# Attention denominators through a row of memory: one broadcast transfer per head instead of four row copies and two shuffles

## The chip, the cores and the metric

The kernel runs on one core of a Trainium2 chip. The metric is the device time of one execution in microseconds (us). A core has five engines that run their own instruction streams and wait for each other through semaphores: TensorE (PE in the profile; its weight loads are PEld), VectorE (DVE), ScalarE (ACT), GpSimd (POOL) and SyncE (SP). In this kernel every transfer is issued by SP, in one queue, and carried by 16 DMA engines.

## The reference

For each batch b and head, queries and keys are projected by `w_phi`, the row's largest absolute value is subtracted, and exp of plus and minus the result gives 256 features:

```python
def phi(x):
    proj = np.einsum('bhsd,df->bhsf', x, w_phi)
    proj = proj - np.max(np.abs(proj), axis=-1, keepdims=True)
    return np.concatenate([np.exp(proj), np.exp(-proj)], axis=-1)
q_p, k_p = (phi(q), phi(k))
kv = np.einsum('bhsf,bhsd->bhfd', k_p, v)
z = np.sum(k_p, axis=2)
num = np.einsum('bhsf,bhfd->bhsd', q_p, kv)
den = np.einsum('bhsf,bhf->bhs', q_p, z)[..., None] + 1e-06
attn = num / den
```

There are 8 batches, 8 heads, 576 positions and a head width of 64. The heads side by side form x, 576 x 512 a batch, which goes through a gated layer: `h = relu(x @ w_in)` (1024 wide), a convolution of width 3 along the positions, a sigmoid of it as the gate, and `(h * gate) @ w_out`. The change concerns the division `num / den` and how its result reaches `x @ w_in`.

## The kernel before

Matrices that need more precision than one pass of TensorE gives are split in a high and a low part (`split`, L56 to L65: the high part by one engine, the rest `src - hi` by another), and a product is three passes.

**Attention.** Heads come in pairs: a tile of 128 partitions holds two heads of 64. A batch has 4 pairs p, two for each half qd of the heads. `k_process` and `q_process` work on groups of columns (five a half, g). The keys' features times v accumulate into `kv`; the queries' features times `kv` give PSUM tiles `nm` of 65 rows, of which 64 are numerators and the 65th is the denominators, because v has a column of ones. ACT copies the numerators to the tile `num` (L459) and the row of denominators to `dr` (L454); a transfer lays that row out as `den`, 72 partitions of 16 (L457): row r of 16 positions of head i stands on partition 2r + i, so that VectorE needs no more than 16 columns for 1152 numbers.

**The division, one process a pair (`x_process`, L464).** VectorE adds 1e-6 (L472) and takes reciprocals into `rc`, 72 x 16 (L473). Then the 576 reciprocals of a head must stand beside each of its 64 partitions of `num`. Four transfers (L477, two a head) write the row of a head to partitions 64i and 64i + 32 of one tile `rr`, which all pairs share. For each chunk c of 290 columns, `stream_shuffle` (L485) spreads the first partition of each 32 over the other 31 into `xf`, which has two buffers, a multiplication by `num` follows (L486), ACT makes the high part `xh` (L60) and VectorE the low part `xl` (L65). There are 8 buffers each of `xh` and `xl`; a new chunk takes one that an earlier part of the gated layer has finished reading.

**Gated layer.** Batch b and chunk c make part n = 2b + c, 16 in all. `h_part` runs 96 matmuls (8 outputs f, 4 pairs, 3 passes) of `xh`, `xl` with `w_in` into `hp`, and ACT applies relu into `h` (L517). `conv_process` does the convolution on POOL (L534) and VectorE (L539), the sigmoid on ACT (L543; it needs another activation table than exp, so a table load of ACT stands before it and before the next exp), the gate product on VectorE (L548), and a split into `gh`, `gl`. `o_part` runs 96 matmuls with `w_out` into `op`; ACT copies them to `os` (L577), which SP stores (L578).

**What sets the order.** The processes are Python generators, and a planner at the end of the function steps attention and gated layer in turn by a clock of its own. That gives the order in which instructions are written down; `tc.high_priority()` moves marked ones ahead. The tile framework then orders each engine's instructions once more by a model of the timeline, places the waits, and each engine runs its list strictly in order. An instruction that waits holds up everything behind it on its engine; a transfer that waits holds up SP's queue. Among the transfers that other work waits for are the rows of maxima `qx<-qmp` (L380), which TensorE's third query pass needs (L386), and the loads `qr`, `kr`, `v`.

Of the kernel before, what the change touches and what calls it, by code (L numbers as in the profile page):

```python
# [7 lines left out]
F32 = mybir.dt.float32  # L8
# [4 lines left out]
ALU = mybir.AluOpType  # L13
AX = mybir.AxisListType.X

B, H, S, D = 8, 8, 576, 64
F = 128
DM, FF = 512, 1024
P = 128
NQ = 2  # L20
TC = 288
HW = TC + 2
# [13 lines left out]
def kernel(  # L36
# [13 lines left out]
    nc = tc.nc  # L50
    cp = ctx.enter_context(tc.tile_pool(name="cp", bufs=1))
    sb = ctx.enter_context(tc.tile_pool(name="sb", bufs=1))
    pg = ctx.enter_context(tc.tile_pool(name="pg", bufs=4, space=bass.MemoryType.PSUM))
    pm = ctx.enter_context(tc.tile_pool(name="pm", bufs=2, space=bass.MemoryType.PSUM))
    pk = ctx.enter_context(tc.tile_pool(name="pk", bufs=1, space=bass.MemoryType.PSUM))

    def split(src, hi, lo, eng_hi, eng_lo):

        if eng_hi is nc.scalar:
            nc.scalar.activation(out=hi, in_=src, func=AF.Copy)  # L60
        elif eng_hi is nc.gpsimd:
            nc.gpsimd.tensor_scalar(out=hi, in0=src, scalar1=1.0, scalar2=0.0, op0=ALU.mult, op1=ALU.add)  # L62
        else:
            nc.vector.tensor_copy(out=hi, in_=src)
        eng_lo.tensor_tensor(out=lo, in0=src, in1=hi.bitcast(F32), op=ALU.subtract)  # L65
# [16 lines left out]
    wq_lo = cp.tile([P, F], F32R, name="wq_lo")  # L82

    wq_m = cp.tile([P, F], F32R, name="wq_m")


    rr = cp.tile([P, S], F32, name="rr")
    nc.gpsimd.memset(rr, 0.0)
    for i in range(2):
        r = slice(D * i, D * i + D)  # L90
        nc.gpsimd.tensor_copy(out=wq_hi[r, :], in_=wbd_hi[r, i * F : (i + 1) * F].bitcast(F32))
    nc.gpsimd.tensor_copy(out=wq_m, in_=rr[:, 0:F])
    nc.gpsimd.tensor_copy(out=wq_lo, in_=rr[:, 0:F])
    nc.gpsimd.tensor_copy(out=wq_lo[0:D, :], in_=wbd_lo[0:D, 0:F].bitcast(F32))
    nc.gpsimd.tensor_scalar(out=wq_m[D : D + 2, :], in0=rr[D : D + 2, 0:F], scalar1=-1.0, scalar2=0.0, op0=ALU.add, op1=ALU.add)
    mx = [cp.tile([32, 32], F32, name=f"mx{i}") for i in range(2)]
    for t in mx:
        nc.gpsimd.memset(t, 0.0)
# [69 lines left out]
    def pe(ns):  # L168
        return ("pe", ns)
# [4 lines left out]
    def until(*keys):  # L174
        return ("until", [k for k in keys if k is not None])

    def set_ready(key, ns=0):
        ready[key] = now[0] + ns * LAT
# [150 lines left out]
    xh, xl = {}, {}  # L329

    def q_process(b, qd, g):
# [129 lines left out]
        if g == 2 or g == 4:  # L461
            spawn(x_process(b, qd * 2 + g // 2 - 1))

    def x_process(b, p):  # L464
        yield ("wait", 4000)
        qd, pr = divmod(p, 2)
        dn, nt = den[b, qd, pr], numt[b, qd, pr]
        if 4 * b + p > 0:
            yield until(("x", *divmod(4 * b + p - 1, 4), 1))
        with tc.high_priority():  # L470
            rc = sb.tile([72, 16], F32, name=f"rc{b}_{p}", tag="rc", bufs=2)
            nc.vector.tensor_scalar(out=dn, in0=dn, scalar1=1e-6, scalar2=None, op0=ALU.add)  # L472
            nc.vector.reciprocal(out=rc, in_=dn)  # L473
            for i in range(2):
                for j in range(2):
                    row = D * i + 32 * j
                    nc.sync.dma_start(out=rr[row : row + 1, :].rearrange("o (r c) -> o r c", c=16),  # L477
                                      in_=rc.rearrange("(r i) c -> i r c", i=2)[i])
        yield ("wait", 4500)
        for c in range(2):  # L480
            yield until(("h", 2 * (b - 1) + c) if b > 0 else None)
            t0 = 0 if c == 0 else S - HW
            with tc.high_priority():
                xf = sb.tile([P, HW], F32, name=f"xf{b}_{p}_{c}", tag="xf", bufs=2)
                nc.vector.stream_shuffle(out=xf, in_=rr[:, t0 : t0 + HW], mask=[0] * 32)  # L485
                nc.vector.tensor_tensor(out=xf, in0=nt[:, t0 : t0 + HW], in1=xf, op=ALU.mult)  # L486
                xh[b, p, c] = sb.tile([P, HW], F32R, name=f"xh{b}_{p}_{c}", tag="xh", bufs=8)
                xl[b, p, c] = sb.tile([P, HW], F32R, name=f"xl{b}_{p}_{c}", tag="xl", bufs=8)
                split(xf, xh[b, p, c], xl[b, p, c], nc.scalar, nc.vector)
            set_ready(("x", b, p, c), 2500)  # L490
            yield pe(125)

# [149 lines left out]
    while moe is not None or chains or active:  # L642
        while chains and sum(1 for p in active if p[2]) < WINDOW:
            b, x, g, kind = chains.pop(0)
# [3 lines left out]
            p = active[-1]  # L648
# [10 lines left out]
        if can_a and (a_first or not can_m):  # L659
            p = active[can_a[0]]  # L660
# [66 lines left out]
```

## Time and profile before

| | |
|---|---|
| median of 3 runs | 825.85 us (825.42 to 827.12) |
| the profiled execution's own time | 827.25 us |
| its span, first to last instruction | 825.5 us |
| mean granted TensorE clock | 0.981 |
| PE busy | 775.8 us, 94% |
| DVE busy | 649.4 us, 79% |
| ACT busy | 627.4 us, 76% |
| POOL busy | 316.1 us, 38% |
| transfers | 55.35 MB by SP's queue, 23.3% of the 16 DMA engines' span |

Busy time is a union over the span, and an engine's share of it is an average over stages: the first 200 us hold the filling of the pipeline and the preparation of the weights, the middle holds attention and gated layer side by side, and from about 720 us only the gated layer is left. "PEclk" is the share of the TensorE clock that was granted. In the trace's rows, `<-` names the tile that is read after the one that is written, and a releaser in brackets is what ended the idle time before an instruction.

### The profile page before, as it was taken

How to read it: one execution, taken by the hardware profiler on the slowest of the kernel's cores; microseconds unless marked ns; L12 is line 12 of the kernel's file. 1: busy time of each engine (PE TensorE's matmuls, PEld its weight loads, DVE VectorE, ACT ScalarE, POOL GpSimd, SP SyncE). 2: the span in 40 equal slices, each digit the busy share in tenths (PEclk: the TensorE clock that was granted, in tenths of full speed). 3: DMA queues.
4: the chain of work that ended last, by engine and by line, in shares of the span. 5: the costliest groups of instructions: out<-in, count | busy, mean ns of one | idle time of the engine just before them, and what ended most of it. 6: DMA issues, size and time to landing. Idle time of an engine off the chain costs nothing. (4 is left out here: it accounts for less than half of the span.)

```text
span 825.5 us, 17295 instructions
## 1 busy us (share of the span) xinstructions
PE 775.8 (94%) x5972; PEld 744.0 (90%) x5972; DVE 649.4 (79%) x1378; ACT 627.4 (76%) x1372; POOL 316.1 (38%) x395
## 2 busy tenths in 40 slices
PE   6988889899999999999999999999999899999997
PEld 5866789798989889999989999999999899999997
DVE  5898999796887968889788798788888587766451
ACT  4787886859898797988888888798988779744322
POOL 5765564262524424344243352525335232211120
PEclk9998989989999999999999999999999899999999
DMA  5544422212222122222222222222222111000001
GB/s 168 179 131 122 130 65 70 66 37 68 67 64 74 38 84 68 68 71 66 78 68 65 69 70 63 70 61 74 62 81 59 51 39 31 10 30 30 22 23 43
DMA packets 66814, 56.44 MB, mean 68 GB/s; under 512 B 17832, under 2 KB 64680, under 8 KB 66728
## 3 DMA queue, kind: packets, MB, share of 16 engines
q1 hardware_dynamic: 66728, 55.35, 23.3%
q8 instruction: 47, 0.77, 0.4%
q14 instruction: 39, 0.32, 0.1%
HBM read 45.21 MB, written 9.44 MB: 66 GB/s over the span
## 5 line engine op out<-in xcount | busy, mean ns | idle before, releaser
L279 PEld LDWEIGHTS kv<-v,ke 128*128 128x128 f32 x1024 | 156.5, 195 | 10.8 <-ACT ke L260 5.2
L279 PE MATMUL kv<-v,ke 128*128 128x65 f32 x1024 | 161.4, 256 | 4.3 <-ACT ke L260 4.2
L539 DVE SCALAR_TENSOR_TENSOR c<-h,cw,c 128x288 f32<-128x288 f32 (+1 forms) x256 | 144.7, 574 | 23.1 <-POOL c L534 21.1
L534 POOL TENSOR_SCALAR c<-h,cw 128x288 f32<-128x288 f32 x128 | 82.3, 645 | 207.2 <-ACT h L517 142.7
L572 PE MATMUL op<-gh,wout_hi 128*128 128x288 f32 x512 | 153.0, 299 | 5.9 <-ACT os L577 5.0
L509 PE MATMUL hp<-xh,win_hi 128*128 128x290 f32 x512 | 154.2, 302 | 4.2 <-ACT h L517 3.3
L572 PE MATMUL op<-gl,wout_hi 128*128 128x288 f32 x512 | 152.3, 298 | 0.9 <-DVE gl L65 0.9
L509 PE MATMUL hp<-xl,win_hi 128*128 128x290 f32 x512 | 153.1, 299 | 0.1
L509 PE MATMUL hp<-xh,win_lo 128*128 128x290 f32 x512 | 152.7, 298 | 0.0
L572 PE MATMUL op<-gh,wout_lo 128*128 128x288 f32 x512 | 152.0, 297 | 0.0
L200 POOL TENSOR_TENSOR qx<-qr,qx 64x512 fp32r<-64x512 f32 (+1 forms) x60 | 77.6, 1294 | 111.2 <-ACT qx L199 102.3
L65 DVE TENSOR_TENSOR ql<-qe,qh 128x512 fp32r<-128x512 f32 x112 | 90.0, 822 | 22.0 <-ACT qh L60 21.7
L509 PEld LDWEIGHTS hp<-xh,win_hi 128*128 128x128 f32 x512 | 97.6, 191 | 7.5 <-ACT h L517 5.4
L572 PEld LDWEIGHTS op<-gh,wout_hi 128*128 128x128 f32 x512 | 97.0, 190 | 7.5 <-ACT os L577 5.9
L572 PEld LDWEIGHTS op<-gl,wout_hi 128*128 128x128 f32 x512 | 97.1, 190 | 1.7 <-DVE gl L65 1.2
L509 PEld LDWEIGHTS hp<-xl,win_hi 128*128 128x128 f32 x512 | 97.9, 191 | 0.7 <-DVE xl L65 0.2
L509 PEld LDWEIGHTS hp<-xh,win_lo 128*128 128x128 f32 x512 | 97.7, 191 | 0.5
L572 PEld LDWEIGHTS op<-gh,wout_lo 128*128 128x128 f32 x512 | 97.2, 190 | 0.5
L62 POOL TENSOR_SCALAR kxh<-kr 128x256 fp32r<-128x256 f32 (+1 forms) x80 | 42.3, 529 | 130.8 <-issue 62.6
L517 ACT ACTIVATE h<-hp 128x290 f32<-128x290 f32 x128 | 50.8, 405 | 40.1 <-PE hp L509 39.6
L432 PE MATMUL nm<-ql,kvh 128*65 128x256 f32 x224 | 69.5, 310 | 0.2 <-DVE ql L65 0.2
L432 PE MATMUL nm<-qh,kvl 128*65 128x256 f32 x224 | 69.2, 309 | 0.0
(99 smaller groups left out, 1879.3 us busy)
## 6 DMA issues: line engine op xcount, KB each, us to landing
qr<-in_qT_dram SPq DMA_DIRECT2D x112, 128.0 KB
v<-in_vt_dram SPq DMA_DIRECT2D x80, 130.0 KB
out_dram<-os SPq DMA_DIRECT2D x64, 144.0 KB
kr<-in_kT_dram SPq DMA_DIRECT2D x64, 128.0 KB
w_r<-in_w_in_dram SPq DMA_DIRECT2D x8, 512.0 KB
w_r<-in_w_out_dram SPq DMA_DIRECT2D x8, 512.0 KB
rr<-rc SPq DMA_DIRECT2D x128, 2.2 KB
qr<-in_qT_dram SPq DMA_DIRECT2D x28, 64.0 KB
```

Of the source, the lines that this page charges most:

```text
L62: nc.gpsimd.tensor_scalar(out=hi, in0=src, scalar1=1.0, scalar2=0.0, op0=ALU.mult, op1=ALU.add)
L65: eng_lo.tensor_tensor(out=lo, in0=src, in1=hi.bitcast(F32), op=ALU.subtract)
L200: nc.gpsimd.tensor_tensor(out=x[D:P], in0=raw[D:P], in1=x[D:P].bitcast(F32), op=ALU.subtract)
L279: ins = nc.tensor.matmul(out=kp[i][:, s, p0 : p0 + VW], lhsT=lhsT, rhs=v[:, (2 * t + i) * VW : (2 * t + i + 1) * VW], start=False, stop=(g ...
L432: ins = after(ins, lambda: nc.tensor.matmul(out=ps[:, i, o : o + w], lhsT=w_, rhs=x_, start=(k == 0), stop=(k == 5)))
L509: nc.tensor.matmul(out=ps, lhsT=w_, rhs=x_, start=(k == 0), stop=(k == 11))
L517: nc.scalar.activation(out=h4[:, f % 4, :], in_=ps, func=AF.Relu)
L534: nc.gpsimd.tensor_scalar(out=cv, in0=hs[:, o : o + TC], scalar1=cw[:, f, 1:2], scalar2=0.0, op0=ALU.mult, op1=ALU.add)
L539: nc.vector.scalar_tensor_tensor(out=cv[:, lo:hi], in0=hs[:, o + j - 1 + lo : o + j - 1 + hi], scalar=cw[:, f, j : j + 1], in1=cv[:, lo:hi ...
L572: nc.tensor.matmul(out=ps, lhsT=w_, rhs=x_, start=(k == 0), stop=(k == 23))
```

## The change

The tile `rr` goes (a tile of zeros for the set-up takes its place there). The reciprocals of a pair are written by one transfer to `rd`, a tile of 2 x 576 in the chip's main memory with two buffers; the address pattern undoes the layout of `rc`, in pieces of 16 numbers. For each head one transfer reads its row back, repeated onto 64 partitions of `rb`, 128 x 576 in SBUF, two buffers. The shuffles go. One multiplication for the whole pair writes `num * rb` into `rb`, and the splits of the two chunks read slices of `rb`.

```diff
-    rr = cp.tile([P, S], F32, name="rr")
+    dp = ctx.enter_context(tc.tile_pool(name="dp", bufs=2, space=bass.MemoryType.DRAM))
+    zero = cp.tile([P, F], F32, name="zero")
...
             nc.vector.reciprocal(out=rc, in_=dn)
+            rd = dp.tile([2, S], F32, name=f"rd{b}_{p}", tag="rd", bufs=2)
+            nc.sync.dma_start(out=rd.rearrange("i (r c) -> r i c", c=16), in_=rc)
+            rb = sb.tile([P, S], F32, name=f"rb{b}_{p}", tag="rb", bufs=2)
             for i in range(2):
-                for j in range(2):
-                    row = D * i + 32 * j
-                    nc.sync.dma_start(out=rr[row : row + 1, :].rearrange("o (r c) -> o r c", c=16),
-                                      in_=rc.rearrange("(r i) c -> i r c", i=2)[i])
+                nc.sync.dma_start(out=rb[D * i : D * i + D, :], in_=rd[i : i + 1, :].broadcast_to([D, S]))
         yield ("wait", 4500)
         for c in range(2):
             yield until(("h", 2 * (b - 1) + c) if b > 0 else None)
             t0 = 0 if c == 0 else S - HW
             with tc.high_priority():
-                xf = sb.tile([P, HW], F32, name=f"xf{b}_{p}_{c}", tag="xf", bufs=2)
-                nc.vector.stream_shuffle(out=xf, in_=rr[:, t0 : t0 + HW], mask=[0] * 32)
-                nc.vector.tensor_tensor(out=xf, in0=nt[:, t0 : t0 + HW], in1=xf, op=ALU.mult)
+                if c == 0:
+                    nc.vector.tensor_tensor(out=rb, in0=nt, in1=rb, op=ALU.mult)
                 xh[b, p, c] = sb.tile([P, HW], F32R, name=f"xh{b}_{p}_{c}", tag="xh", bufs=8)
                 xl[b, p, c] = sb.tile([P, HW], F32R, name=f"xl{b}_{p}_{c}", tag="xl", bufs=8)
-                split(xf, xh[b, p, c], xl[b, p, c], nc.scalar, nc.vector)
+                split(rb[:, t0 : t0 + HW], xh[b, p, c], xl[b, p, c], nc.scalar, nc.vector)
```

Because the framework orders the instructions anew, they move on every engine. Three places follow. A name such as `xh_1_0_9527` is pair 1, chunk 0 of its batch and then the tile's own number (the batch is left out); the changed file is one line longer at the top, so L66 there is the L65 of before and L61 the L60. In brackets stand the semaphores that the instruction waits for; those named DMAHW belong to transfers.

**ScalarE, batch 6, pairs 0 and 1**, where their chunks are split. Before:

```order
1017 L60 ACTIVATE xh_0_0_9220<-xf_0_0_9217 128x290 [waits PE_49]
1018 L60 ACTIVATE xh_0_1_9227<-xf_0_1_9224 128x290 [waits PE_49]
1019 L517 ACTIVATE h_4_8675<-hp_7_8705 128x290 [waits PE_49]
1020 L60 ACTIVATE xh_1_0_9527<-xf_1_0_9524 128x290 [waits DVE_49]
1021 L371 ACTIVATE qmt_0_2_9272<-qmt_0_2_9272 32x16 [waits DVE_49]
1022 L371 ACTIVATE qmt_0_2_9272<-qmt_0_2_9272 32x16 x2
1023 L60 ACTIVATE xh_1_1_9534<-xf_1_1_9531 128x290 [waits DVE_49]
1024 L543 ACT_TABLE_LOAD
1025 L543 ACTIVATE c_9068<-c_9068 128x2304 [waits DVE_49]
1026 L399 ACT_TABLE_LOAD
```

Now:

```order
1027 L61 ACTIVATE xh_0_0_9125<-rb_0_8937 128x290 [waits PE_49]
1028 L399 ACTIVATE qe_0_2_0_9528<-qp_0_2_9171 128x512 [waits DVE_49]
1029 L61 ACTIVATE xh_0_1_9129<-rb_0_8937 128x290 [waits PE_49]
1030 L61 ACTIVATE xh_1_0_9428<-rb_1_9244 128x290 [waits PE_49]
1031 L399 ACTIVATE qe_0_2_1_9532<-qp_0_2_9171 128x512 [waits DVE_49]
1032 L61 ACTIVATE xh_1_1_9432<-rb_1_9244 128x290 [waits PE_49]
1033 L517 ACTIVATE h_4_8581<-hp_7_8611 128x290
1034 L260 ACTIVATE ke_1_1_9424<-ks_1_1_9422 128x512 [waits DVE_49]
1035 L261 ACTIVATE ke_1_1_9424<-ks_1_1_9422 128x512
1036 L199 ACTIVATE qx_1_0_9470<-qr_1_0_9467 128x256 [waits DMAHW3_49,DMAHW0_49,DMAHW4_49,PE_49,Pool_49]
1037 L543 ACT_TABLE_LOAD
```

Pair 1's two splits waited for VectorE; now they wait for TensorE alone, as pair 0's do (VectorE's count that they need has been waited for by then), and four other instructions stand between the last split and the table load for the sigmoid, where none did.

**SyncE, batch 2, pair 0.** Before, the four transfers of the reciprocals and what is behind them:

```order
188 L457 DMA den_0_0_2509<-dr_0_2_2683 32x1x16 [waits DMAHW3_49,Activation_49]
189 L477 DMA rr<-rc_0_3362 1x36x16 [waits DMAHW4_49,DVE_49]
190 L477 DMA rr<-rc_0_3362 1x36x16 [waits DMAHW5_49]
191 L477 DMA rr<-rc_0_3362 1x36x16 [waits DMAHW6_49]
192 L477 DMA rr<-rc_0_3362 1x36x16 [waits DMAHW7_49]
193 L380 DMA qx_1_0_2492<-qmp_1_0_2639 2x8x32 [waits DMAHW0_49,DVE_49,PE_49]
```

Now:

```order
180 L380 DMA qx_0_4_2309<-qmp_0_4_2587 2x16x32 [waits DMAHW3_49,DVE_49]
181 L476 DMA rd_0_3335<-rc_0_3332 36x2x16 [waits DMAHW4_49,DVE_49]
182 L479 DMA rb_0_3337<-rd_0_3335 64x576 [waits DMAHW5_49,DMAHW4_49]
183 L479 DMA rb_0_3337<-rd_0_3335 64x576 [waits DMAHW6_49]
184 L380 DMA qx_1_0_2470<-qmp_1_0_2618 2x8x32 [waits DMAHW7_49,DVE_49,PE_49]
```

Three transfers stand where four stood, and the first read waits for DMAHW4, the semaphore of the write just ahead of it: SP cannot go on before the write has landed, and a `qx` is next. In 6 of the 32 pairs the read follows the write directly like this; in the others 1 to 21 transfers stand between them. For two pairs of batch 4 and all pairs from batch 5 on, the first read also waits for VectorE, for the buffer of the pair two earlier.

**VectorE, batch 2, pair 1**, from the reciprocal to its first use. Before:

```order
371 L473 RECIPROCAL rc_1_3673<-den_0_1_2515 72x16
372 L539 SCALAR_TENSOR_TENSOR c_3404<-h_4_3011,cw,c_3404 128x287
373 L539 SCALAR_TENSOR_TENSOR c_3404<-h_4_3011,cw,c_3404 128x288
374 L65 TENSOR_TENSOR xl_0_0_3557<-xf_0_0_3553,xh_0_0_3556 128x290
375 L375 TENSOR_REDUCE mx_90<-qmt_1_2_2794 32x16
376 L376 TENSOR_REDUCE qm_1_2_2799<-qmt_1_2_2794 32x16
377 L65 TENSOR_TENSOR xl_0_1_3564<-xf_0_1_3560,xh_0_1_3563 128x290
378 L377 TENSOR_TENSOR mx_90<-qm_1_2_2799,mx_90 32x16
379 L539 SCALAR_TENSOR_TENSOR c_3404<-h_4_3011,cw,c_3404 128x287
380 L379 STREAM_TRANSPOSE qmp_1_2_2803<-mx_90 32x32
381 L539 SCALAR_TENSOR_TENSOR c_3404<-h_4_3011,cw,c_3404 128x288
382 L485 STREAM_SHUFFLE xf_1_0_3860<-rr 128x290
```

Now:

```order
347 L473 RECIPROCAL rc_1_3639<-den_0_1_2493 72x16
348 L375 TENSOR_REDUCE mx_92<-qmt_1_2_2768 32x16
349 L376 TENSOR_REDUCE qm_1_2_2773<-qmt_1_2_2768 32x16
350 L539 SCALAR_TENSOR_TENSOR c_3375<-h_4_2981,cw,c_3375 128x288
351 L377 TENSOR_TENSOR mx_92<-qm_1_2_2773,mx_92 32x16
352 L379 STREAM_TRANSPOSE qmp_1_2_2777<-mx_92 32x32
353 L66 TENSOR_TENSOR ql_1_1_2864<-qe_1_1_0_2865,qh_1_1_2863 128x512
354 L66 TENSOR_TENSOR ql_1_1_2864<-qe_1_1_1_2869,qh_1_1_2863 128x512
355 L486 TENSOR_TENSOR rb_1_3644<-num_0_1_2494,rb_1_3644 128x576
```

Ten instructions stood between the reciprocal and the first shuffle; seven stand now between it and the multiplication.

More of the change, by code (lines that the diff above doesn't have):

```diff
@@ L84 @@
     wq_m = cp.tile([P, F], F32R, name="wq_m")
-    rr = cp.tile([P, S], F32, name="rr")
-    nc.gpsimd.memset(rr, 0.0)
+    zero = cp.tile([P, F], F32, name="zero")
+    nc.gpsimd.memset(zero, 0.0)
     for i in range(2):
@@ L91 @@
         nc.gpsimd.tensor_copy(out=wq_hi[r, :], in_=wbd_hi[r, i * F : (i + 1) * F].bitcast(F32))
-    nc.gpsimd.tensor_copy(out=wq_m, in_=rr[:, 0:F])
-    nc.gpsimd.tensor_copy(out=wq_lo, in_=rr[:, 0:F])
+    nc.gpsimd.tensor_copy(out=wq_m, in_=zero)
+    nc.gpsimd.tensor_copy(out=wq_lo, in_=zero)
     nc.gpsimd.tensor_copy(out=wq_lo[0:D, :], in_=wbd_lo[0:D, 0:F].bitcast(F32))
-    nc.gpsimd.tensor_scalar(out=wq_m[D : D + 2, :], in0=rr[D : D + 2, 0:F], scalar1=-1.0, scalar2=0.0, op0=ALU.add, op1=ALU.add)
+    nc.gpsimd.tensor_scalar(out=wq_m[D : D + 2, :], in0=zero[D : D + 2, :], scalar1=-1.0, scalar2=0.0, op0=ALU.add, op1=ALU.add)
     mx = [cp.tile([32, 32], F32, name=f"mx{i}") for i in range(2)]
```

## The prediction, made before the changed kernel was run

> **What bounds the kernel now.** I read the busy times of the page first, then busy time by stage, then who waits for whom.
>
> ```profile
> PE 775.8 (94%) x5972; PEld 744.0 (90%) x5972; DVE 649.4 (79%) x1378; ACT 627.4 (76%) x1372; POOL 316.1 (38%) x395
> ```
>
> The four stages, in the columns PE, PEld, DVE, ACT, POOL, granted clock, share of the DMA engines, GB/s:
>
> ```profile
> 0.00:200.00 200.00, 173.79 (x1230) 157.62 (x1231) 169.65 (x333) 150.44 (x320) 105.78 (x128) 0.94 0.36 104
> 200.00:300.00 100.00, 93.15 (x747) 89.29 (x746) 84.15 (x186) 84.92 (x192) 37.99 (x49) 1.00 0.23 65
> 300.00:720.00 420.00, 408.03 (x3254) 397.17 (x3253) 343.53 (x777) 353.40 (x800) 159.03 (x194) 0.99 0.22 62
> 720.00:825.50 105.50, 100.88 (x748) 99.87 (x746) 52.12 (x84) 38.64 (x63) 13.29 (x24) 1.00 0.09 29
> ```
>
> TensorE sets the end. Its idle time is 825.5 - 775.8 = 49.7 us: 26.2 in the first 200 us, 6.9 to 300, 12.0 to 720, 4.6 after. The change takes nothing from TensorE, so it can win only in those 49.7 us and in the stretches at a lower clock, and in the last stage it finds nothing. VectorE is 85% busy in the first stage and 82% in the third: loaded, but second. What TensorE waits for (total us, times, longest) shows how far VectorE reaches it:
>
> ```profile
> PE op L572 <- ACT os L577: 5.0, 3, 4.2
> PE qp L386 <- DMA qx<-qmp: 3.4, 4, 1.4
> PE tp L353 <- DVE qs L230: 1.6, 2, 1.0
> PE op L572 <- DVE gl L65: 0.9, 1, 0.9
> PE nm L432 <- DVE ks L230: 0.6, 1, 0.6
> PE nm L420 <- DVE ks L230: 0.5, 1, 0.5
> ```
>
> VectorE ends 3.6 us of waits directly (the last four rows). The rest it reaches through ScalarE, and there one place is this change's own. ScalarE's waits have a row for it, and its timeline in batch 6, with VectorE's beside it, shows the longest case:
>
> ```profile
> ACT xh L60 <- DVE xf L486: 7.5, 5, 2.7
> ```
>
> ```profile
> 633.31 0.45 ACT L60 ACTIVATE xh<-xf 128x290 fp32r<-128x290 f32 x1 [2.70 <-DVE xf L486]
> ...
> 635.09 1.28 ACT L543 ACT_TABLE_LOAD   x1
> 636.38 2.13 ACT L543 ACTIVATE c<-c 128x2304 f32<-128x2304 f32 x1
> 638.53 1.28 ACT L399 ACT_TABLE_LOAD   x1
> ...
> 642.96 0.41 ACT L577 ACTIVATE os<-op 128x288 f32<-128x288 f32 x1
> ```
>
> ```profile
> 630.90 0.81 DVE L65 TENSOR_TENSOR xl<-xf,xh 128x290 fp32r<-128x290 f32 x2
> ...
> 631.65 0.47 DVE L485 STREAM_SHUFFLE xf<-rr 128x290 f32<-128x290 f32 x1
> ...
> 632.83 0.44 DVE L486 TENSOR_TENSOR xf<-num,xf 128x290 f32<-128x290 f32 x1
> ```
>
> ScalarE stands idle for 2.70 us before pair 1's `xh`, because pair 1's shuffle cannot start before pair 0's `xl` gives back a buffer of `xf` (two for all pairs). Everything behind it is late, the sigmoid and the copy `os` too, and TensorE waits for that copy:
>
> ```profile
> 643.42 0.61 PE L572 MATMUL op<-gh,wout_hi 128*128 128x288 f32 x1 [4.18 <-ACT os L577]
> ```
> ```profile
> 640.00:645.00 5.00, 1.58 (x6) 1.58 (x7) 2.04 (x5) 4.87 (x14) 1.56 (x1) 0.70 0.05 12
> 645.00:650.00 5.00, 5.00 (x25) 4.86 (x25) 1.96 (x3) 0.86 (x3) 0.00 (x0) 0.62 0.23 76
> ```
>
> The clock falls after it: 5 x 0.30 + 5 x 0.38 = 3.4 us of full speed lost in these 10 us. The place costs 4.2 + 3.4 = 7.6 us.
>
> **The change part by part.** The sum goes against the profiled execution's 827.25 us (span 825.5 and 1.75 around it), 1.4 above the median of 825.85; I subtract it from both.
>
> *The stall in batch 6.* `rb` has two buffers of a whole pair, and in the changed order (shown above) pair 1's split waits for TensorE's release alone, its multiplication being done by then. So the 2.70 us go, and the gap of 4.18 falls to about 1.5. What remains is ScalarE's own: two table loads and a sigmoid, 1.28 + 2.13 + 1.28. Whether the clock then holds, these rows bound from both sides:
>
> ```profile
> 415.00:425.00 10.00, 8.54 (x69) 8.01 (x68) 8.74 (x20) 6.62 (x20) 4.58 (x7) 1.00 0.06 15
> 48.00:60.00 12.00, 10.02 (x58) 8.21 (x56) 11.25 (x24) 9.53 (x22) 7.32 (x8) 0.86 0.52 150
> ```
>
> 1.5 us of idle at 415 left it at 1.00; 2.0 us at 48, in two pieces, took it to 0.86. A gap of 1.5 is nearer the first; I take half of the 3.4. Term: -2.7 - 1.7 = -4.4, between 0 (another instruction of ScalarE's is late in its place) and -7.6.
>
> The Trainium skill's page TensorE: Matmul & The Clock Gate, Part 1, says that an idle window of about 3.4 us of a free-running counter halves the clock. By that, 1.5 us would spare the clock wholly and the term would be -6.1. The row at 48 does not agree, since 2.0 us of idle were enough there.
>
> *VectorE's work.* The shuffles go, and 64 multiplications become 32 twice as wide:
>
> ```profile
> L486 DVE TENSOR_TENSOR xf<-num,xf 128x290 f32<-128x290 f32 x64 | 29.6, 482 | 0.0
> L485 DVE STREAM_SHUFFLE xf<-rr 128x290 f32<-128x290 f32 x64 | 29.1, 483 | 0.0
> L548 DVE TENSOR_TENSOR c<-c,h 128x1152 f32<-128x1152 f32 x32 | 43.7, 1405 | 14.8 <-ACT c L543 14.8
> ```
>
> From 482 ns at 290 columns and 1405 at 1152 it is 1.07 ns a column, so 576 columns take 482 + 286 x 1.07 = 788 ns, and 32 of them 25.2 us. VectorE loses 29.1 + 29.6 - 25.2 = 33.5 us, 5% of its work. Nearly all lies beside TensorE's work. On TensorE's path it can give at most the 3.6 us above, at least nothing; a twentieth less work does not clear a queue, so I take about a quarter, -1.0.
>
> *The way through memory.* SP's timeline and VectorE's in batch 3 price the old way:
>
> ```profile
> 303.89 3.11 SPq L477 DMA_DIRECT2D rr<-rc  x4
> 307.11 0.45 SPq L578 DMA_DIRECT2D out_dram<-os  x1
> ```
> ```profile
> 308.23 0.01 DVE L485 LOAD_MASK_SELECT xf<-rr  x1 [1.89 <-DMA rr<-rc]
> ```
>
> From the first issue to the shuffle 4.34 us; the last of four issues (0.78 each) began at 306.2, so one transfer lands 2.0 us after its issue begins. The new way is a write and then two reads. The write has 72 pieces of 64 bytes against 36: I take 2.0 for it as well. A store of 144 KB to memory, issued at 822.32, ended SP's last wait at 822.65 + 1.4:
>
> ```profile
> 822.32 0.33 SPq L578 DMA_DIRECT2D out_dram<-os  x1
> SPq L722 <- DMA out_dram<-os: 1.4, 1, 1.4
> ```
>
> that is 1.7 us, so memory as target need not be slower. A read is 64 x 2304 bytes, 147 KB; the nearest rows are loads of keys, 128 KB, each issue with POOL's start on it:
>
> ```profile
> 7.36 0.85 SPq L203 DMA_DIRECT2D kr<-in_kT_dram  x2
> 9.65 0.41 POOL L62 TENSOR_SCALAR kxh<-kr 128x256 fp32r<-128x256 f32 x1 [2.88 <-DMA kr<-in_kT_dram]
> 10.97 0.33 SPq L203 DMA_DIRECT2D kr<-in_kT_dram  x1
> 15.15 0.43 POOL L62 TENSOR_SCALAR kxh<-kr 128x256 fp32r<-128x256 f32 x1 [3.02 <-DMA kr<-in_kT_dram]
> ```
>
> 2.3 us, and 4.2 when the DMA engines are loaded. Two reads 0.5 apart: 2.8. Together 2.0 + 2.8 = 4.8 us, 0.5 more than now; the bounds are 1.7 + 2.3 = 4.0 and 2.0 + 0.5 + 4.2 = 6.7. Behind the waiting multiplication stands all of VectorE's queue. It waits so today in seven cases:
>
> ```profile
>   DMA rr<-rc: 8.2, 7
> ```
>
> With half a microsecond more and, as in the order for batch 2, less work between reciprocal and use, I expect these waits to double to some 16 us. That is a quarter of the relief given back: +0.6, between 0 and +3.6 (TensorE's direct waits for VectorE doubled).
>
> The page DMA: Bandwidth & Descriptors of the Trainium skill, in Latency and other measured facts, speaks against the change: memory takes 0.2 us on average but 2 us under high load, and the receipt of the write is most of a transfer's fixed cost. By that each round trip in the first 100 us would be about 2 us longer; for four pairs, all stalling VectorE, an estimate of at most +8 instead of +0.6. The trace has no small write to memory to test it.
>
> *SP's queue.* Four issues held SP 3.1 us a pair. Now: one issue (0.78), the landing of the write if nothing stands between (2.0 - 0.78 = 1.2), two issues of the kind of `kr` or `out` (0.33 to 0.45 each): 2.8 at most. Term 0, as long as the reads' waits for a buffer end early. Bytes: 32 x 295 KB = 9.4 MB on the 55.35 MB of the queue, whose share is
>
> ```profile
> q1 hardware_dynamic: 66728, 55.35, 23.3%
> ```
>
> so some 27% instead of 23%: 0.
>
> **Sum:** -4.4 - 1.0 + 0.6 = -4.8: 827.25 to 822.4 for an execution like the profiled one, 825.85 - 4.8 = **821** as the time of the runs.
>
> **The rivals.**
> *Nothing that counts.* The stall in batch 6 is replaced: the two table loads and the sigmoid (4.7 us) stay in ScalarE's queue, and any instruction before them that waits for VectorE keeps the gap. The waits for `rb` eat the rest. For it: 33 us of relief meet only 3.6 us of waits. Against: the reason for the 2.70 us is gone from the order. Time: 825.85 within 0.2%, 824.2 to 827.5; 0.2% is about what a measurement of this kernel can tell from no change.
> *SP is held, and the third query pass comes late: slower.* A read waits for the write, or from batch 4 on for `xl` of two pairs earlier, which itself waits for TensorE; the `qx` transfer is next in line, TensorE needs it, and it already has 3.4 us of waits for it in four cases. It decides once SP stands more than a microsecond beyond today's 3.1 us: if that reaches TensorE with 1.2 us for eight of the 32 pairs, 9.6 us, less the 1.0 of relief and with the stall replaced, the time is 834; with half of them, 830. For it: SP stands today for the shared row,
>
> ```profile
> SPq L477 <- DVE xf L486: 17.9, 6, 6.1
> ```
>
> and with that only 3.4 us reach TensorE; against: two buffers make this wait rarer.
> *More than forecast: the first stage moves too.* There TensorE idles 26.2 us and the clock is 0.94 (12 us lost); VectorE does about 1 us less a pair for eight pairs. If the first stage gets back a fifth of those 38 us, 7.6, the time is 821 - 7.6 = 813.
>
> **How the numbers follow.** Forecast (817 to 824, its own range) 0.47; more than that 0.11; no difference 0.18; slower 0.24. So faster 0.58, same 0.18, slower 0.24. Since the order moves on every engine, single stalls of 2 to 8 us can come and go on both sides; the range reaches from the third rival's 813 to 831, in the lower half of the second's, and leaves out about 2 in 10.
>
> **What would show it.** Right: ScalarE's waits before `xh` for VectorE (7.5 us now) near zero, no gap of 4 us before `os`, the clock at 1.00 from 300 to 720 us; VectorE busy near 616 us; the multiplication 0.7 to 0.8 us; VectorE's waits for the reads 10 to 20 us. Wrong: SP's waits for the write or for `rb` large with TensorE's waits for `qx` above 8 us (the second rival), or a new gap over 3 us at another copy of ScalarE's (the first). The forecast falls if TensorE's busy time changes by more than 5 us, since nothing in it says so.

## The result: 2.5% slower

The changed kernel takes 847.83 us (the median of four runs: three took 845.87 to 848.55, and one, at a granted clock of 0.843, took 859.38 and is left out of the ratio), the kernel before 826.43 beside it on the same chip: a ratio of 1.0252, 95% interval 1.0226 to 1.0278. The forecast of 821 and its range of 813 to 831 were both missed, and on the wrong side.

The page of the changed kernel, its busy times:

```profile
PE 780.9 (93%) x5972; PEld 745.2 (88%) x5972; DVE 627.0 (74%) x1218; ACT 628.2 (74%) x1372; POOL 322.8 (38%) x395
```

The same stages as before, in the same columns (PE, PEld, DVE, ACT, POOL, clock, DMA share, GB/s):

```profile
0.00:200.00 200.00, 172.81 (x1231) 156.15 (x1231) 167.25 (x290) 149.96 (x316) 106.26 (x126) 0.96 0.39 114
200.00:300.00 100.00, 90.67 (x702) 87.67 (x703) 74.83 (x160) 79.56 (x182) 38.70 (x50) 0.97 0.26 77
300.00:720.00 420.00, 398.12 (x3158) 383.34 (x3157) 323.15 (x676) 351.20 (x794) 158.52 (x189) 1.00 0.26 74
720.00:844.10 124.10, 119.30 (x885) 118.08 (x884) 61.81 (x94) 47.44 (x82) 19.32 (x32) 0.99 0.10 32
```

VectorE has 22 us less to do, and TensorE stands idle for 63.2 us where it was 49.7. By stage that is 27.2 (26.2 before), 9.3 (6.9), 21.9 (12.0) and 4.8 (4.6): the middle stage lost most, where VectorE became freer. At 720 us TensorE has 119 us of work left instead of 101. Beside 13.5 us more of idle time, TensorE is busy 5.1 us longer with as many matmuls (780.9 against 775.8); the runs don't show where these come from.

Who waits for whom, by the groups of waits:

```profile
DVE rb L486 <- DMA rb<-rd: 30.6, 23, 3.5
...
DVE den L472 <- DMA den<-dr: 22.5, 13, 2.8
...
PE qp L386 <- DMA qx<-qmp: 9.7, 9, 2.5
...
PE nm L432 <- ACT num L459: 5.1, 2, 5.0
...
PE op L572 <- ACT os L577: 1.3, 1, 1.3
...
ACT xh L61 <- DVE rb L486: 0.7, 1, 0.7
```

The kernel before, where it differs and was not shown:

```profile
DVE den L472 <- DMA den<-dr: 5.6, 8, 1.0
```

VectorE now waits 30.6 us for the broadcast rows (8.2 us for `rr` before). It also waits 22.5 us for the denominators, 17 more than before, although the change leaves that transfer as it was. ScalarE's waits before `xh` are all but gone, and the gap of 4.18 us before `os` in batch 6 with them. But a new gap stands 80 us earlier, at the sigmoid of another part. TensorE and then ScalarE there, in their timelines:

```profile
566.80 0.48 PE L432 MATMUL nm<-qh,kvh 128*65 128x256 f32 x1 [4.97 <-ACT num L459]
```
```profile
559.95 0.66 ACT L371 ACTIVATE qmt<-qmt 32x16 f32<-32x16 f32 x3 [4.24 <-DVE qmt L368]
...
562.57 1.28 ACT L543 ACT_TABLE_LOAD   x1
563.87 2.12 ACT L543 ACTIVATE c<-c 128x2304 f32<-128x2304 f32 x1
...
566.30 0.44 ACT L459 ACTIVATE num<-nm 64x64 f32<-64x64 f32 x2
```

ScalarE waited 4.24 us for a reduction of VectorE's (`qmt`). In VectorE's timeline it had stood still for the denominators 2.84 us, and then worked for 7 us almost without a pause before the turn of the reduction came:

```profile
551.96 0.17 DVE L472 TENSOR_SCALAR den<-den 72x16 f32<-72x16 f32 x1 [2.84 <-DMA den<-dr]
...
559.21 0.71 DVE L368 TRANSPOSE_TENSOR_REDUCE qmt<-qp 128x16 f32<-128x512 f32 x1
```

The last experiment below takes the waits for the denominators away, and a gap of 4.15 us stays at this place, so they are not what makes it.

The new way itself, at a pair where nothing is in the way: SP's timeline, then VectorE's.

```profile
186.70 0.79 SPq L476 DMA_DIRECT2D rd<-rc  x1
188.64 1.15 SPq L479 DMA_DIRECT2D rb<-rd  x2
```
```profile
192.17 0.76 DVE L486 TENSOR_TENSOR rb<-num,rb 128x576 f32<-128x576 f32 x1 [0.34 <-DMA rb<-rd]
```

From the write's issue to the multiplication 5.5 us, where the old way took 4.3.

### The profile page after: what moved, and what is told of

Its sections match the earlier page's. It is cut to its first block, busy times and chain, and to the rows that moved or that the text cites. A ratio compares the mean times of both kernels' runs of the same rounds, so it can differ in the third digit from the quotient of the medians.

```text
span 844.1 us, 17158 instructions
## 1 busy us (share of the span) xinstructions
PE 780.9 (93%) x5972; PEld 745.2 (88%) x5972; DVE 627.0 (74%) x1218; ACT 628.2 (74%) x1372; POOL 322.8 (38%) x395
## 4 chain that ended last, share of the span: by engine, by line
PE 33%; ACT 14%; DVE 8%; DMA 6%; issue 3%; POOL 2%; SPq 1%; ACTq 0%; POOLq 0%; DVEq 0%
PE op L572 13%; PE hp L509 11%; PE nm L432 3%; PE kv L279 3%; DMA den<-dr 3%; DVE c L539 2%; ACT qe L399 2%; ACT qh L61 2%; ACT num L459 2%; ACT dr L454 1%; DVE ql L66 1%; ACT qmt L371 1%; POOL qx L200 1%; DVE qmt L368 1%; DMA rb<-rd 1%
## 5 line engine op out<-in xcount | busy, mean ns | idle before, releaser
L534 POOL TENSOR_SCALAR c<-h,cw 128x288 f32<-128x288 f32 x128 | 91.0, 714 | 206.1 <-ACT h L517 120.6
L539 DVE SCALAR_TENSOR_TENSOR c<-h,cw,c 128x288 f32<-128x288 f32 (+1 forms) x256 | 151.6, 603 | 23.1 <-POOL c L534 21.0
L66 DVE TENSOR_TENSOR ql<-qe,qh 128x512 fp32r<-128x512 f32 x112 | 86.0, 786 | 30.7 <-ACT qh L61 30.4
L432 PE MATMUL nm<-qh,kvh 128*65 128x256 f32 x224 | 63.3, 284 | 6.9 <-ACT num L459 5.1
```

The source lines that it names most:

```text
L432: ins = after(ins, lambda: nc.tensor.matmul(out=ps[:, i, o : o + w], lhsT=w_, rhs=x_, start=(k == 0), stop=(k == 5)))
L534: nc.gpsimd.tensor_scalar(out=cv, in0=hs[:, o : o + TC], scalar1=cw[:, f, 1:2], scalar2=0.0, op0=ALU.mult, op1=ALU.add)
L539: nc.vector.scalar_tensor_tensor(out=cv[:, lo:hi], in0=hs[:, o + j - 1 + lo : o + j - 1 + hi], scalar=cw[:, f, j : j + 1], in1=cv[:, lo:hi ...
```

## The experiments

The times are medians; "before" is always the kernel before, timed beside them (825.99 to 827.82 us). Four theories stood at the start. W: VectorE, and all that is queued behind it, stands still for the longer way through memory. B: the bytes of the broadcast reads hold up other transfers. O: the order that the framework made anew costs the time, whatever the way. S: SP is held, the second rival of the prediction.

### Four kernels that take the way apart

**A constant row.** The same transfers and bytes, but the reads take rows of q. No read waits for the write, and so none for the reciprocals; the division is not by the denominators.

```diff
-in_=rd[i : i + 1, :].broadcast_to([D, S])
+in_=qT[0, 0, i : i + 1, 0:S].broadcast_to([D, S])
```

> The changed kernel, but the two reads of a pair take two fixed rows of the input q in memory instead of the row just written: the write, the broadcast bytes, the multiplication and the splits stay, the round trip behind the reciprocal is gone (so the division is not by the denominators). Theory W (VectorE stands in its queue until write and reads have landed, 30.6 us in 23 cases, and what is behind it is late): VectorE's waits for the reads fall under 5 us and the time to 822 to 830. Theory B (9.4 MB more bytes and broadcast reads slow the other transfers): 843 to 849, since the bytes are the same. Theory O (the framework's new order alone, attention ahead of the gated layer): 840 to 849.

Measured: 828.87 us, ratio 1.0034 (1.0015 to 1.0053). 19 of the 21 us are back with the same 9.4 MB of reads, so the bytes are not the cause. Its waits of VectorE for the rows:

```profile
DVE rb L486 <- DMA rb<-in_qT_dram: 4.3, 6, 0.9
```

VectorE's relief is worth nothing here that the time shows: all of the saved shuffles are in this kernel, nothing waits for the way through memory, and it is not faster than the kernel before. It has an order of its own, though.

**Rows in on-chip memory, work on whole pairs.** The old four transfers into two row tiles in turn; one shuffle in place and one multiplication of 576 columns a pair.

```diff
+            rr = rrs[p % 2]
...
+                if c == 0:
+                    nc.vector.stream_shuffle(out=rr, in_=rr, mask=[0] * 32)
+                    nc.vector.tensor_tensor(out=rr, in0=nt, in1=rr, op=ALU.mult)
```

> The kernel before with the second half of the change alone: the rows stay in SBUF (four transfers as before), but into two tiles in turn, and one shuffle and one multiplication of 576 columns a pair, in place. Theory W: the trip is as short as before and VectorE has about 8 us less to do, so 820 to 827. Theory B: 820 to 827. Theory O (a new order costs, whatever the waits): could lie anywhere from 822 to 845.

Measured: 848.35 us, ratio 1.0282 (1.0239 to 1.0325), as slow as the changed kernel with VectorE waiting only 14.2 us for the rows, and above every expectation. This does not fit a theory in which waits for memory alone hold the time.

**The same through memory, without broadcast.** One write, two reads of both rows, then the shuffle.

```diff
+            nc.sync.dma_start(out=rd.rearrange("i (r c) -> r i c", c=16), in_=rc)
+            for j in range(2):
+                nc.sync.dma_start(out=rr[32 * j : 32 * j + D + 1 : D, :], in_=rd)
```

> As the kernel with one shuffle and one multiplication a pair, but the rows go through memory: one write, then two reads of 2 x 2.3 KB to the first partitions of the four groups of 32, no broadcast. Against that kernel only the round trip is longer (about 5 us instead of 4.2) and two transfers fewer. Theory W: VectorE's waits for the rows 20 to 30 us, time 835 to 846. Theory B: the bytes are gone, 822 to 829. Theory O: no forecast.

Measured: 839.2 us, ratio 1.0157 (1.0111 to 1.0202). The time is theory W's, its waits are not: VectorE waits 5.0 us for the rows, not 20 to 30, and 19.1 us for the denominators. With the longer way this kernel is 9 us faster than the one above with the short way, so among kernels that work on whole pairs the length of the way does not decide alone.

**The kernel before with one more hop**, on-chip memory to on-chip memory, ahead of its four row transfers.

```diff
             nc.vector.reciprocal(out=rc, in_=dn)
+            rh = sb.tile([72, 16], F32, name=f"rh{b}_{p}", tag="rh", bufs=2)
+            nc.sync.dma_start(out=rh, in_=rc)
```

> The kernel before with one more transfer in the chain, from SBUF to SBUF: the reciprocals are first copied to another tile, and the four row transfers read the copy. It adds a landing of about 2 us to each pair's trip and one issue to SP, no bytes worth naming, nothing in memory. Theory W: VectorE's waits for the rows rise from 8 to 25 us or more and the time to 834 to 846. Theory B: 825 to 828. Theory S (SP stands for the landing and holds the transfers behind it): as theory W, with TensorE's waits for the maxima above 8 us.

Measured: 844.38 us, ratio 1.0231 (1.0193 to 1.0269). The hop landed 1.95 us after its issue (median of 32). Two more microseconds on the way make the old kernel nearly as slow as the new one, without memory and without the new multiplication. Again the time is theory W's, but VectorE waits 10.3 us for the rows, not 25 or more, and 17.2 us for the denominators; TensorE's waits for the maxima are 6.0 us, below the 8 of theory S. But each of the four also has an order of its own on every engine. Waits and order had to be told apart.

### The order held fixed

A kernel is built twice. From the first build each engine's order is read; in the second, a dependency for the order alone (no semaphore) ties each instruction to its predecessor in that order:

```diff
+    for u, w in zip(ranks, ranks[1:]):
+        tc.add_manual_dep(mine[w], mine[u].name, DependencyInfo(DependencyClass.NoSync, ...))
```

**The changed kernel, TensorE in the order of before.**

> The changed kernel with all its work, but TensorE runs its 5,200 matmuls in exactly the order that they have in the kernel before; the other engines are ordered anew around that. Theory W (VectorE and what is queued behind it stand still for the longer way through memory): the way is as long as before this edit, so the time stays with the changed kernel, 840 to 852 us. Theory O (the time is set by the order that the framework finds, and the order of before happens to be a good one): most of the loss goes, 822 to 832 us.

Measured: 841.36 us, ratio 1.0175 (1.0139 to 1.0211), as theory W had it. The longer way is paid in TensorE's old order too; VectorE waits 39.2 us for the rows.

**The constant row, in exactly the changed kernel's order, SP's too.**

> The changed kernel, whose two reads a pair take rows of q from memory in place of the row just written (so it doesn't divide by the denominators), and every engine and SP's queue keep exactly the order that the changed kernel has. What goes is the wait of the reads for the landing of the write; the reads still stand behind the write in SP's queue, which waits for the reciprocal. The way gets about 1 to 1.5 us shorter of 5.4 to 5.9. Theory W: 832 to 842 us, a share of the loss like the share of the way that goes. Theory O: 842 to 850 us.

Measured: 840.96 us, ratio 1.0179 (1.0138 to 1.0221), just inside theory W's range. VectorE's waits for the rows fell from 30.6 to 22.8 us, and the time by 6.9: nearly one for one.

**The row ahead, in exactly the order of the changed kernel's four engines.**

> As the constant row with the order kept (the division is again not by the denominators), but only TensorE, VectorE, ScalarE and GpSimd keep exactly the changed kernel's order; the reads of the row may be issued ahead, so that the multiplication doesn't wait for them at all. VectorE's wait in front of the multiplication (30.6 us in the changed kernel) should fall under 5 us. Theory W: 820 to 832 us. Theory O: 838 to 850 us.

Measured: 841.59 us, ratio 1.0182 (1.0148 to 1.0215), in theory O's range. Its waits:

```profile
DVE den L481 <- DMA den<-dr: 22.7, 14, 3.9
...
DVE rb L513 <- DMA rb<-in_qT_dram: 8.6, 10, 2.8
```

The waits for the way fell by 22 us, to 8.6 (under 5 was expected), and the time by 6.2. But this test has a delay of its own. SP's order is not kept, and four reads of the row, with loads that stood behind it, now stand ahead of the load of `cw_raw`, which VectorE needs early. SP and TensorE's first `kv`, in the changed kernel:

```profile
5.80 0.43 SPq L142 DMA_DIRECT2D cw_raw<-in_conv_w_dram  x1
```
```profile
9.52 1.23 PE L275 MATMUL kv<-v,ke 128*128 128x130 f32 x4 [1.00 <-ACT ke L260]
```

And here:

```profile
11.49 0.43 SPq L151 DMA_DIRECT2D cw_raw<-in_conv_w_dram  x1
```
```profile
14.95 1.23 PE L284 MATMUL kv<-v,ke 128*128 128x130 f32 x4 [6.16 <-ACT ke L269]
```

VectorE waits 9.9 us for `cw_raw` in place of 4.4, and TensorE is 5.4 us late from the start. From this matmul to the end of the span it is 834.6 us in the changed kernel and 824.6 here. So in the changed kernel's own order the waits for the new way are worth 6 us of the 21, and up to 10 if nothing of that delay was made up for later; a part may be SP's new order, since TensorE's waits for `qx` are 5.8 us here against 9.7. The other 11 to 15 come with an order in which little of the way is left to wait for. The waits for the denominators are still there: they belong to the order.

**The kernel before with the hop, its four engines in exactly their old order.**

> The kernel before with one more transfer, from on-chip memory to on-chip memory, between the reciprocal and its four row transfers, so that the way is some 2 us longer; TensorE, VectorE, ScalarE and GpSimd keep exactly the order of the kernel before. With an order of its own this kernel took 844.4 us. Theory W: 836 to 848 us, as long as with the order of its own. Theory O: 824 to 832 us.

Measured: 852.64 us, ratio 1.0332 (1.0268 to 1.0396), above both expectations and worse than with an order made for the hop (844.38). So "the order alone" fails as well: in the order of before, two more microseconds of way cost 26 us. Its busy TensorE, and VectorE's waits:

```profile
PE 787.3 (92%) x5972; PEld 752.9 (88%) x5972; DVE 649.6 (76%) x1378; ACT 628.3 (74%) x1372; POOL 320.1 (38%) x395
```
```profile
DVE xf L510 <- DMA rr<-rh: 36.8, 16, 4.4
```

**The changed kernel in the order of the constant row** (TensorE, ScalarE, GpSimd).

> The changed kernel with all its work, but TensorE, ScalarE and GpSimd keep exactly the order that the framework found for the kernel with the constant row (828.9 us there), where no read waits for the reciprocal; VectorE and SP are ordered anew. If the waits for the way through memory cost no more than they do in the changed kernel's own order (6 us, 847.8 against 841.6), 833 to 838 us, and the rest of the loss lies in the order. If an order that was found without the way is upset by it, as the order of before was by the hop (852.6 us), 845 to 860 us.

Measured: 921.2 us, ratio 1.1142 (1.1102 to 1.1182), far beyond both expectations. This order took 828.87 us where nothing waits for the way. With the real way TensorE stands before the gated layer:

```profile
DVE rb L513 <- DMA rb<-rd: 56.6, 25, 6.1
PE hp L536 <- ACT xh L65: 39.9, 5, 9.6
```

So an order that is good where nothing waits is bad for the real way, as the order of before is for the hop. The framework makes one for the longer way, and that limits the loss to 21 us; it does not find one that hides it.

### Other orders of the same work

One constant of the planner changes the order and no work: `AHEAD` (how far the later batches' attention is moved ahead), or the pause of 4,500 behind the transfers in `x_process`. Theory D: the old kernel's order was a lucky draw, and any new one costs 10 to 20 us. Theory M: the longer way makes the framework's orders worse.

```diff
-AHEAD = 300
+AHEAD = 400
```

> The kernel before with the same work and one constant changed, AHEAD 400 in place of 300, by which the framework orders the work anew: 2,249 of TensorE's 5,200 matmuls stand elsewhere, the first at number 880. Theory D (the order of before is a lucky draw, and any other order of the same work costs 10 to 20 us): 835 to 848 us. Theory M (orders found for the short way are all about as good, and it is the longer way that makes them worse): 822 to 832 us.

> The same with AHEAD 200: 2,983 of the matmuls stand elsewhere, the first at number 832. Theory D: 835 to 848 us. Theory M: 822 to 832 us, though a change of a constant that gives the attention less precedence can have an effect of its own.

> The changed kernel with AHEAD 200 in place of 300 and nothing else: 3,528 of its matmuls stand elsewhere. Theory D: anywhere from 826 to 852 us, since it is a new draw. Theory M: 838 to 852 us, since the longer way is there as before.

> The changed kernel with AHEAD 400 in place of 300 and nothing else; the kernel before took 821.3 us with this constant. Pairs so far: 844.8 before and 845.3 after with AHEAD 200, 826.4 and 847.8 with AHEAD 300. Theory D (the order is a draw of 821 to 848 us for either kernel): anywhere from 821 to 848 us, with no fixed distance to 821.3. Theory M (the longer way makes the order worse): 838 to 848 us, 17 to 27 us above 821.3.

> The changed kernel with reads of rows of q (no read waits for the reciprocal, and the division is not by the denominators), and AHEAD 400. With AHEAD 300 it took 828.9 us. Theory M: without the way it is again 10 to 25 us faster than the changed kernel of the same constant, 818 to 830 us. Theory D: a new draw, 821 to 848 us, on either side of the changed kernel's.

> The kernel before with the same work and the planner's own pause behind the row transfers at 3,000 in place of 4,500, by which 3,755 of the 5,200 matmuls stand elsewhere. Theory D: a third draw of the same work, anywhere from 821 to 848 us. Theory M: 820 to 835 us.

> The changed kernel with the same pause at 3,000; 3,170 matmuls stand elsewhere. Theory D: no fixed distance to the kernel before with that pause, and either may be the faster. Theory M: 10 to 25 us slower than the kernel before with that pause.

Measured, in us, with the constant row and the whole-pair kernel where they were run (the kernels of a row in part on different chips, where the kernel before took 825.99 to 827.82):

| order | before | changed | difference | constant row | whole pairs, rows on chip |
|---|---|---|---|---|---|
| AHEAD 300 | 826.43 | 847.83 | +21.4 | 828.87 | 848.35 |
| AHEAD 200 | 844.79 | 845.33 | +0.5 | | |
| AHEAD 400 | 821.26 | 843.57 | +22.3 | 821.48 | 839.66 |
| pause 3,000 | 833.16 | 850.45 | +17.3 | | |

The same work takes 821 to 845 us by its order alone, so theory M's bound for the old kernel (822 to 832) was too tight, and AHEAD 200 makes the two kernels alike. But the changed kernel lies at 844 to 850 in all four, and comes within 20 us of the best old order in none. Theory D, by which any other order of the old work costs 10 to 20 us, falls with the 821.26 of AHEAD 400. That the changed kernel's loss is nothing but a worse draw is unlikely after four settings, though they do not exclude it. The constant row, with its bytes and VectorE's relief but no way, is with the kernel before under both constants; under AHEAD 400 it is 22 us faster than the changed kernel. In the kernel before with the pause at 3,000 VectorE waits 21.0 us for the denominators, about as long as in the changed kernel (22.5), and it is 7 us slower than with 4,500: such waits come up in an order made for the short way as well.

AHEAD 400 with the old kernel beats both kernels of this case: 821.26 us, ratio 0.9934 (0.9907 to 0.9962). Its page:

```profile
PE 771.4 (94%) x5972; PEld 740.5 (90%) x5972; DVE 654.7 (80%) x1378; ACT 628.3 (77%) x1372; POOL 320.2 (39%) x395
```

TensorE is busy 4.4 us less than before with the same matmuls, and VectorE is busier than in any other kernel here.

### Whole pairs, and the waits for the denominators

**The whole-pair kernel again, with AHEAD 400.**

> The kernel with the rows in on-chip memory (the short way of the kernel before, two row tiles in turn) and one shuffle and one multiplication a pair, with AHEAD 400; with AHEAD 300 it took 848.35 us although its way is short. If what slows it is its draw of the order, as with the kernel before at AHEAD 200 (844.8 us), 820 to 834 us here. If it is the work on whole pairs (the tile that is held until both halves are split, and the first half that waits for a multiplication of 576 columns), 840 to 850 us again, and then this is a cause of the changed kernel's loss beside the way.

Measured: 839.66 us, ratio 1.0133 (1.0098 to 1.0167), a hair under the lower edge for "whole pairs" and 6 us above the other range. Under both constants, working on whole pairs is slow too as long as the rows come from the denominators, even by the short way.

**The row ahead, the changed kernel's order, and no wait for the denominators.** The division is again not by them.

```diff
-    nc.vector.tensor_scalar(out=dn, in0=dn, scalar1=1e-6, scalar2=None, op0=ALU.add)
+    nc.vector.tensor_scalar(out=rc, in0=one, scalar1=1e-6, scalar2=None, op0=ALU.add)
```

> The kernel with the row ahead and the changed kernel's order kept on TensorE, VectorE, ScalarE and GpSimd (841.6 us), and now VectorE's addition of 1e-6 reads a constant in place of the denominators, so that it doesn't wait for their transfers either (22.7 us in all there, 5.6 us in the kernel before); the division is not by the denominators. If these waits, which the order puts in front of VectorE, are what makes the order slow, 826 to 835 us. If they cost nothing, because TensorE doesn't wait for what is behind them, 839 to 843 us, and the loss lies in the order of the other engines, as the gap of 5 us behind the sigmoid does.

Measured: 834.85 us, ratio 1.0093 (1.006 to 1.0127), at the upper edge of the first expectation: another 7 us. By stage:

```profile
0.00:200.00 200.00, 169.39 (x1230) 152.64 (x1231) 167.59 (x289) 148.90 (x315) 103.42 (x126) 0.97 0.40 116
200.00:300.00 100.00, 91.71 (x722) 88.26 (x721) 78.09 (x164) 82.85 (x188) 40.92 (x51) 0.98 0.28 79
300.00:720.00 420.00, 406.57 (x3235) 394.43 (x3234) 329.31 (x685) 355.74 (x804) 159.44 (x192) 0.99 0.26 74
```

In the middle stage TensorE is idle 13.4 us, against 21.9 in the changed kernel and 12.0 before: the two kinds of VectorE's waits explain nearly all that was lost there. The gap at the sigmoid belongs to the order and stays:

```profile
555.14 0.48 PE L442 MATMUL nm<-qh,kvh 128*65 128x256 f32 x1 [4.15 <-ACT num L469]
```

So with the changed kernel's order held, of 21 us 6 to 10 are waits for the new way and some 7 are waits for the denominators that this order puts in front of VectorE. What is left holds the delay at the start again: TensorE's first `kv` starts at 15.19 us here. From there to the end of the span it is 816.3 us, and 816.2 in the kernel before (from 9.29 us). So beside VectorE's waits in it, this order may cost nothing at all; how much of the delay was made up for later, the runs don't show.

## Why the prediction was wrong

*The stall in batch 6 (-4.4): right about the place, wrong about the sum.* ScalarE's wait before `xh` went from 7.5 us to 0.7 and the gap of 4.18 is gone, as foretold. But a gap of 4.97 us came at the sigmoid of another part. The forecast's lower bound of 0 described this ("another instruction of ScalarE's is late in its place"); the value taken did not.

*VectorE's work (-1.0): mis-sized twice, harmless.* The multiplication took 815 ns against 788. VectorE's busy time fell by 22.4 us instead of 33.5, because other lines became slower (below). What this relief gives TensorE is nothing measurable: the constant row, in orders of its own, has it all and is 0.2 us slower than the old kernel under AHEAD 400, 2.9 us under AHEAD 300.

*The way through memory (+0.6, at most +3.6): the step that failed.* Its length was within the bounds, 5.5 us against a forecast of 4.8 and bounds of 4.0 to 6.7. VectorE's waits for it became 30.6 us, not 16. The fault was the bound: I let the harm reach TensorE only by its direct waits for VectorE, 3.6 us, doubled. The hop in the fixed old order shows how far that is off: 2 us more way, VectorE's waits up by 28.6 us, the time by 26. In the changed kernel's own order, 22 us less of these waits gave back 6 to 10 us, and 7.8 us less gave back 6.9. VectorE's standstill is passed on to everything that waits for anything behind it in its list, on whichever engine. The row that should have warned was VectorE at 82 to 85% busy, with ScalarE and, through `qx`, SP and TensorE waiting for its small reductions; the chain at 552 to 566 us above shows that reach.

*The order: a term that was not there.* I took the new order as noise of "single stalls of 2 to 8 us" on both sides, and read its three places as improvements. In fact 11 to 15 us of the loss come with the order that the framework makes for the changed kernel. Some 7 of them are shown to be waits of VectorE's that this order brings: it meets the denominators too early (22.5 us of waits against 5.6). The rest stays open, and may be no more than the delay at the start of the two tests. That such an order follows from the longer chain from the denominators to the finished halves, by transfer or by work on whole pairs, fits the hop, the constant row and the whole-pair kernels; it is argued from them, not shown. Against it, among whole-pair kernels the one with the longer way was the faster, and the kernel before with the pause at 3,000 has these waits by the short way. The kernel before at AHEAD 200 is as slow with 7.5 us of them, so there are other ways to a bad order.

*SP's queue (0): right in size.* Summed over their transfers, the time from the producer's end to the issue fell, for `qx` from 42.7 to 25.9 us and for `den` from 125.4 to 110.6.

*The rivals.* The second, "SP is held, and the third query pass comes late", came nearest with its sign and its 834, and half of its mark was met: TensorE's waits for `qx` are 9.7 us, above 8. Its mechanism was not: SP stands 10.3 us for the writes, and still issued the `qx` transfers sooner after their producers than before. TensorE's busy time, which the forecast said must not move by more than 5 us, moved by 5.1.

## What to carry to other kernels

Where a scheduler orders in-order engines around a modelled timeline, price a longer dependency not by the waits at its end but by an experiment with the delay alone: an extra hop in the old kernel cost 18 us with an order made for it and 26 in the old order, where the whole change cost 21. Before a difference of 2% is put down to an edit, run the same work in two or three other orders; here one constant moved it by 23.5 us, more than the edit did. Work taken from an engine that is not the bound (here 22 us of VectorE) bought nothing measurable, while a microsecond or two more of what that engine waits for, in each of 32 pairs, cost about 20. And a test that holds the order must hold the transfer queue's order too, or look at what the free queue did: here it may have hidden up to 5 us.

## What the runs showed of the hardware

The same instruction got slower without any change of its own. VectorE's 256 convolution steps, before and then changed, from the groups by line (busy us, mean ns, idle before):

```profile
L539 DVE SCALAR_TENSOR_TENSOR c<-h,cw,c 128x288 f32<-128x288 f32 (+1 forms) x256 | 144.7, 574 | 23.1 <-POOL c L534 21.1
```
```profile
L539 DVE SCALAR_TENSOR_TENSOR c<-h,cw,c 128x288 f32<-128x288 f32 (+1 forms) x256 | 151.6, 603 | 23.1 <-POOL c L534 21.0
```

That is 6.9 us more, most of what VectorE's saving came short by. It is 568 ns in the kernel before with AHEAD 400, so the mean moves from kernel to kernel with the same steps. What does this was not tried.

The longer gap cost less clock. After 4.18 us of idle TensorE the kernel before ran at 0.70 and 0.62 for 10 us, 3.4 us lost; after 4.97 us the changed kernel ran as follows (columns as in the stages above):

```profile
561.00:567.00 6.00, 1.03 (x8) 0.80 (x7) 5.25 (x11) 5.85 (x10) 0.00 (x0) 0.94 0.32 98
567.00:575.00 8.00, 8.00 (x59) 7.90 (x59) 3.59 (x8) 6.10 (x13) 1.95 (x3) 0.83 0.20 57
```

6 x 0.06 + 8 x 0.17 = 1.7 us. Both gaps exceed the idle window of about 3.4 us of which the Trainium skill speaks (TensorE: Matmul & The Clock Gate, Part 1), and both lost clock, so the rule holds for these two as to whether (the prediction's row at 48 us, with 2.0 us of idle in two pieces, is a loss below that window); as to how much, the two gaps differ by a factor of two.

Memory as a stop on the way was cheap: a write of 72 small pieces landed 1.97 us after its issue began (median of 32), against 1.95 for the hop's transfer of as many pieces to on-chip memory and 1.82 for a row transfer. The 2 us extra per round trip under load that I had estimated from the Trainium skill (DMA: Bandwidth & Descriptors, Latency and other measured facts) did not come at this load (DMA engines 51% busy in the first 110 us): in that time the four pairs' reads landed 2.9 to 4.3 us after their issue, against a median of 3.06 over all.
